# Four shared key neighbours, resident end blocks and whole-array value products in a sparse-attention and channel-mix kernel

## The chip, the cores and the metric

The kernel runs on one core of one Trainium2 chip. The metric is device time in microseconds (us) of one execution. The engines are named as in the profile: PE is TensorE (PEld its weight loads), DVE VectorE, ACT ScalarE, POOL GpSimd, SP SyncE, whose queue issues nearly all DMAs here.

## The reference

Inputs are `q`, `k`, `v` (4 batches, 8 heads, 768 positions, 64 channels, float32), three sampled key blocks for each of 24 query blocks of 32 positions, and the weights of a channel mixer.

```python
scores = (1 / np.sqrt(D)) * np.matmul(q, k.transpose(0, 1, 3, 2))
mask = np.abs(blk_i - blk_j) <= 1                       # a block and its neighbours
mask = mask | (blk_i == 0) | (blk_j == 0) | (blk_i == 23) | (blk_j == 23)
for qb in range(24):
    for kb in sampled_blocks[qb]:
        mask[qb*32:(qb+1)*32, kb*32:(kb+1)*32] = True
attn = softmax(np.where(mask, scores, -1e9)); x = attn @ v       # heads side by side: 512 channels
x_prev = x shifted by one position
xk = mu_k * x + (1 - mu_k) * x_prev;  xr = mu_r * x + (1 - mu_r) * x_prev
k = np.maximum(xk @ w_k, 0.0)                            # 512 -> 1024
out = sigmoid(xr @ w_r) * ((k * k) @ w_v)                # 1024 -> 512
```

The three weight matrices arrive as float64 and are taken apart on the chip.

## The kernel before, in words

Attention is done in 24 units (`UNITS`). Four of them are wide (`ALL`): for one batch, 128 queries of blocks 21, 22, 23 and 0 (the first and last block attend to everything, the others ride along under a mask) against all 768 keys. Twenty are near units `(pr, m)`: for a pair of batches, two neighbouring query blocks n = 2m+1 and n+1, so again 128 query rows (2 batches x 2 blocks x 32), each against 8 key blocks: its three window blocks, the first and the last block, and its three sampled blocks.

A wide unit goes head pair by head pair (`wide_pair`, four of them): scores of two heads (`sw`, L577, two row halves of the array side by side, 384 keys at a time), a fused mask-add-and-minimum on DVE (L494), an exponential on ACT (L504), twelve 128x128 transposes on PE (`tw`, L515), copied out four at a time (`ptw`, on ACT, L519), and the product with the values (L599). That product runs as four column tiles: for each of the 6 key chunks and each 32 queries there is a matmul of its own, with 32 stationary columns and the same 64 moving columns of values. Each float32 matmul is two PE instructions and two weight loads in the trace.

A near unit (`near_group`, twice, four heads each) does the same with 64x32 tiles for scores (`s`, L538), transposes (`t`, L515, copied out by DVE, L521) and 128x32 tiles for values (`o`, L560), where the four column tiles do have different values. `finish` divides by the sum (L621), transposes (`tx`, L618), and writes into `xt`, the mixer's input, by tiles of 256 positions.

Keys of a near unit sit in two tiles `KR0` and `KR1` of 8 blocks, one for each query block: three window blocks by one DMA from `kd` (L466), the two ends when the batch pair changes (L461), three sampled blocks by a DMA each from `kt` (L463). Both halves of the unit's scores read both tiles, so there is no second set to load into ahead of time. Values sit in a ring of six `VR` tiles of four blocks: for each query block a tile from `vw` (window and first block in one host-made table, L485) and one with the last block and the three sampled ones (`vt`, L480 and L482). A wide unit takes three of the same ring for its 768 keys (L440).

The mixer works on 12 tiles of 256 positions (`TILES`): `gate` (`r`, L744), `hidden` (`h_0`..`h_3`, L762), `values` (`v`, L791) as matmuls in three float32r terms of split operands; splitting is done on POOL, DVE and ACT (`split_x`, L707 to L720; `hidden`, L775 to L779). The 20 weight pieces are loaded on ACT's queue, rebuilt by ACT and three DVE steps (L360 to L373) and split on POOL (L383, L387).

Nothing of this runs in the order written. Every operation is added to a `Plan` with an engine, a cost in ns, a rank (a due time worked out from constants such as `A_STEP`, `M_STEP`, `O_PV`) and what it reads and writes. `Plan.order` simulates the engines with these costs and places at each step the operation with the lowest rank among those that can start soon; then everything is issued in that one order, and each engine's queue runs in order. Costs therefore decide the order, never the work. PE has modes in the plan: `whole`, `wide` (row halves), `scores` and `values` (small tiles), with a price `LEAVE` for leaving each. Where the plan sees a gap on PE of at least 150 ns before 95 us, it issues idle matmuls there (`spin`, L334, tile `idle`).

Of the kernel before, what the change touches and what calls it, by code (L numbers as in the profile page):

```python
# [29 lines left out]
QB, SLOTS = 4, 8  # L30
PAIR = 2
# [49 lines left out]
class Op:  # L81
    __slots__ = ("engine", "ns", "lag", "fn", "rank", "deps", "users", "bufs", "end", "start", "table", "seq", "waits", "release", "size", "parts", "ready")


class Plan:


    HOP = {"PE": 260, "ACT": 100, "DVE": 170, "POOL": 170, "SP": 60}
# [3 lines left out]
    RING, RATE, DONE, LANES = 650, 300, 670, 8  # L92
# [7 lines left out]
    def add(self, engine, ns, rank, fn, reads=(), writes=(), lag=0, table=None, release=0.0, size=0, parts=1):  # L100
# [5 lines left out]
        op.bufs, op.release, op.size, op.parts = [], release * 1000, size, parts  # L106
# [30 lines left out]
    def order(self):  # L137
        free, table, avail = {}, {}, {}
        queue_free = 0.0
        lanes, lane = [0.0] * self.LANES, 0  # L140
        for op in self.ops:
# [6 lines left out]
        while len(placed) < len(self.ops):  # L148
            best = None
            for engine, ops in avail.items():  # L150
                now = free.get(engine, 0.0)
                cand = []
                for op in ops:
                    at = max(now, op.ready)
                    for buf in op.bufs:
                        if not buf.taken:
                            slots, times, queue = self.queues[buf.tag]
                            if queue[0] is not buf or not times:
                                at = None
                                break  # L160
                            at = max(at, min(times)[0])
                    if at is not None:
                        cand.append((at, op))
# [25 lines left out]
            free[op.engine] = op.end  # L189
            for buf in op.bufs:  # L190
# [9 lines left out]
            for u in op.users:  # L200
                u.waits -= 1
                if not u.waits:
                    u.ready = max([u.release] + [d.end + (self.HOP[d.engine] if d.engine != u.engine else self.SAME.get(u.engine, 60)) + d.lag
                                                 for d in u.deps])
                    avail.setdefault(u.engine, []).append(u)
# [9 lines left out]
    (2, ALL), (0, ALL), (1, ALL), (0, 0), (0, 1), (0, 2), (0, 3), (3, ALL), (0, 4), (0, 5), (0, 6), (0, 7),  # L215
# [14 lines left out]
def block_sparse_attention_channel_mix(  # L230
    ctx: ExitStack, tc: tile.TileContext,
    kt, kd, kq, qw, qn, vt, vw, blocks, rows, consts, mu_k, mu_r, w_k, w_v, w_r, out, wide,
# [22 lines left out]
    KR = [fixed([P, SLOTS, PAIR, HP * BLK], F32, f"KR{i}") for i in range(KR_BUFS)]  # L255
# [11 lines left out]
    def mask_setup():  # L267
        own = buf([P, NM + 1, NRAND, 2], I32, "kk", 3, "own")
        con = buf([P, NM * (SEEN + SLOTS) + 2 * NB], F32, "zr", 3, "con")
        f = buf([P, NM + 1, NRAND], F32, "dif", 2, "ownf")  # L270
        same = buf([P, NM * NRAND * SEEN], F32, "x0", 1, "same")
# [18 lines left out]
        plan.add(DVE, 600, -15, pack, reads=[(number,)], writes=[(word,), (packed,)])  # L290
# [14 lines left out]
        def twice():  # L305
# [4 lines left out]
            e = same.ap.rearrange("p (a i b) -> p a i b", i=NRAND, b=SEEN)  # L310
# [3 lines left out]
            v.tensor_reduce(out=near_mask.ap[:, :, SEEN:], in_=e, axis=AX.X, op=ALU.max)  # L314
            d = same.ap[:, 0:NM].unsqueeze(2)
            for i, j in ((1, 0), (2, 0), (2, 1)):
                v.tensor_tensor(out=d, in0=g[:, :, i : i + 1], in1=g[:, :, j : j + 1], op=ALU.is_equal)
                m = near_mask.ap[:, :, SEEN + i : SEEN + i + 1]
                v.tensor_tensor(out=m, in0=m, in1=d, op=ALU.max)
            m = near_mask.ap[:, :, SEEN:]  # L320
            v.tensor_scalar(out=m, in0=m, scalar1=-FAR, scalar2=None, op0=ALU.mult)

        plan.add(DVE, 1100, -30, far, reads=[(own,), (con,)], writes=[(f,), (same,), (wide_mask,)])
        plan.add(DVE, 2400, TWICE, twice, reads=[(f,), (con,)], writes=[(same,), (near_mask,)])
# [20 lines left out]
    def weight(i, owner, key, dst, src, rank):  # L345
        f = buf([P, 512], F32, "zr", 3, f"wf{i}")
        if wide:
# [11 lines left out]
            else:  # L359
                plan.add(ACT, 600, rank, lambda: nc.scalar.activation(  # L360
# [16 lines left out]
            plan.add(DVE, 340, rank, shift, reads=[(mag,)], writes=[(mag,)])  # L377
            plan.add(DVE, 602, rank, sign, reads=[(mag,), (raw,)], writes=[(mag,)])
            plan.add(DVE, 602, rank, tail, reads=[(mag,), (raw,)], writes=[(f,)])
        else:  # L380
            plan.add(SP, ISSUE, rank, lambda: nc.sync.dma_start(f.ap, src), writes=[(f,)], size=262144)
        if i in HI_POOL:
            plan.add(POOL, 700, rank, lambda: nc.gpsimd.tensor_copy(dst()[:, 0, :], f.ap), reads=[(f,)], writes=[(owner, (0, key))])  # L383
        else:
            plan.add(ACT, 520, rank, lambda: nc.scalar.copy(dst()[:, 0, :], f.ap), reads=[(f,)], writes=[(owner, (0, key))])
        plan.add(POOL, 1230, rank,
# [20 lines left out]
    taken = [0, 0]  # L407

    def place(ring):

        taken[ring] += 1
        return (taken[ring] - 1) % (KR_BUFS, VR_BUFS)[ring]
# [7 lines left out]
    def load_wide(b, at):  # L420
# [13 lines left out]
        for i in range(NB // QB // 2):  # L434
            w = place(1)
# [9 lines left out]
    def load_near(pr, m, at):  # L445
# [4 lines left out]
        keys, values = [], []  # L450
        ahead = FIRST_K if (pr, m) == (0, 0) else LEAD_K
        for j in range(PAIR):
            n = PAIR * m + 1 + j
            r = place(0)
            keys.append(r)
            more = slots[0][r] != pr
            slots[0][r] = pr

            def fetch(r=r, n=n, more=more):
                if more:  # L460
                    nc.sync.dma_start(KR[r].ap[:, 3:5].rearrange("p n b x -> p n (b x)"), kt[pr * NB : (pr + 1) * NB : NB - 1].rearrange("n p x -> p n x"))  # L461
                for i in range(NRAND):
                    nc.sync.dma_start(KR[r].ap[:, 5 + i].rearrange("p b x -> p (b x)"),  # L463
                                      kt[bass.ds(sampled_block(n, i) + pr * NB, 1)].rearrange("o p x -> p (o x)"))

            plan.add(SP, ISSUE, at - ahead + 0.01 * j, lambda r=r, n=n: nc.sync.dma_start(  # L466
                KR[r].ap[:, 0:3].rearrange("p n b x -> p (n b x)"), kd[pr, :, n - 1 : n + 2].rearrange("p n x -> p (n x)")),
                writes=[(KR[r], "near")], release=at - ahead, size=393216)
            plan.add(SP, NRAND * FETCH + FIND * (pr == 0) + ISSUE * more, at - ahead + 0.01 * j, fetch, reads=[(packed,)],
                     writes=[(KR[r], "far")], release=at - ahead, size=131072 * (NRAND + 2 * more), parts=NRAND + more)  # L470
        for j in range(PAIR):
            n = PAIR * m + 1 + j
            near, far = place(1), place(1)
            values.append((near, far))
            more = slots[1][far] != pr
            slots[1][near], slots[1][far] = None, pr

            def gather(w=far, n=n, more=more):
                if more:
                    nc.sync.dma_start(VR[w].ap[0:BLK].rearrange("p b x -> p (b x)"), vt[(pr + 1) * NB - 1].rearrange("k b x -> k (b x)"))  # L480
                for i in range(NRAND):
                    nc.sync.dma_start(VR[w].ap[(i + 1) * BLK : (i + 2) * BLK].rearrange("p b x -> p (b x)"),  # L482
                                      vt[bass.ds(sampled_block(n, i) + pr * NB, 1)].rearrange("o k b x -> (o k) (b x)"))
# [3 lines left out]
            plan.add(SP, NRAND * FETCH + ISSUE * more, at - LEAD_V + 0.01 * j, gather, reads=[(packed,)],  # L487
                     writes=[(VR[far], 0, 1)], release=at - LEAD_V, size=131072 * (NRAND + more), parts=NRAND + more)
        return q, keys, values
# [13 lines left out]
    def exp(p, cs, keys, nm, col, L, h, rank):  # L503
        plan.add(ACT, 280 + 0.83 * (cs.stop - cs.start), rank, lambda: nc.scalar.activation(  # L504
# [3 lines left out]
    def turn(parts, name, rank, act=False):  # L508
# [9 lines left out]
        if act:  # L518
            plan.add(ACT, 490, rank + 0.1, lambda: nc.scalar.copy(pt.ap, tp.ap), reads=[(tp,)], writes=[(pt,)])  # L519
        else:  # L520
            plan.add(DVE, 600, rank + 0.1, lambda: nc.vector.tensor_copy(out=pt.ap, in_=tp.ap), reads=[(tp,)], writes=[(pt,)])  # L521
# [3 lines left out]
    ROWS = [slice(i * BLK, (i + 1) * BLK) for i in range(QB)]  # L525

    def near_group(b, m, gi, q, keys, values, o, L, t0):

        s = buf([P, 2, 512], F32, "s", 2, f"s{b}_{m}_{gi}", ps)
        p = buf([P, 4 * 256], F32, "p", P_BUFS, f"p{b}_{m}_{gi}")  # L530
        nm = buf([P, 4], F32, "nm", 4, f"nm{b}_{m}_{gi}")

        def mm():
            for a in range(2):
                hp = 2 * gi + a
                for j in range(QB):
                    for row, half in enumerate(HALF):
                        nc.tensor.matmul(  # L538
                            s.ap[ROWS[j], row, a * 256 : (a + 1) * 256].rearrange("p (n x) -> p n x", x=BLK),
                            q.ap[half, hp, ROWS[j]], KR[keys[j % PAIR]].ap[half, :, j // PAIR, hp * BLK : (hp + 1) * BLK],  # L540
                            start=True, stop=True, skip_group_check=True)

        plan.add(PE, 920, t0, mm, reads=[(q, 2 * gi, 2 * gi + 1), *[(KR[r], "near", "far") for r in keys]], writes=[(s,)], table="scores")
# [405 lines left out]
```

## Time and profile before

| | |
|---|---|
| median of 3 runs | 623.88 us (622.9 to 626.05) |
| the profiled execution | 623.73 us, span 622.0 us |
| PE busy | 589.5 us of the span, with 30.7 us of `idle` matmuls among them |
| DVE, ACT, POOL busy | 291.8, 301.0, 287.1 us |
| mean granted TensorE clock | 0.983 |
| DMA | 108.55 MB, mean 175 GB/s |

The busy time of PE counts an instruction to its modelled end, and consecutive matmuls overlap, so a group is best read from the start of its first instruction to the start of the next group, as the chain of waits gives it. Times of single instructions are longer than their share of a run of them: a 128x256 matmul of the mixer has a mean of 285 ns, and 24 of them take 3 us.

### The profile page before, as it was taken

The numbers are of one execution on the slowest core, as the hardware profiler recorded it, in microseconds if no ns is written. First come the engines' busy times: TensorE is split into PE (matmuls) and PEld (weight loads), VectorE is DVE, ScalarE is ACT, GpSimd is POOL, SyncE is SP. The second block draws the span as 40 slices with busy tenths as digits, with TensorE's granted clock in tenths as the row PEclk, the third lists the DMA queues.
The fourth block names the chain that finished last, engine by engine and source line by source line (L and its number), as shares of the span: only waits on it lengthen the run. The fifth ranks groups of instructions, "written<-read, shape, count | busy, mean of one in ns | idle before, by whom it ended". The sixth has DMA issues, their size and how long they took to land.

```text
span 622.0 us, 20533 instructions
## 1 busy us (share of the span) xinstructions
PE 589.5 (95%) x8267; PEld 479.7 (77%) x8281; DVE 291.8 (47%) x850; ACT 301.0 (48%) x716; POOL 287.1 (46%) x360
## 2 busy tenths in 40 slices
PE   9998898697989999899999999999999999999997
PEld 4666675465776897687887978979889788989896
DVE  5676764466688444734344343454343452312200
ACT  4676761356476355536273473554454554243341
POOL 1122411105475541564553653735617547496751
PEclk9999999799889999999999999999999999999999
DMA  8995799788679756885447447684384320000000
GB/s 323 337 322 195 212 246 261 214 284 280 190 208 279 239 144 174 264 228 153 167 141 224 124 132 214 182 265 136 111 257 136 120 79 2 35 17 18 18 18 34
DMA packets 54992, 108.55 MB, mean 175 GB/s; under 512 B 9681, under 2 KB 26706, under 8 KB 54898
## 3 DMA queue, kind: packets, MB, share of 16 engines
q1 hardware_dynamic: 51730, 96.63, 51.7%
q10 hardware_dynamic: 3168, 10.61, 5.1%
q8 instruction: 65, 1.06, 0.7%
q14 instruction: 29, 0.24, 0.1%
HBM read 100.40 MB, written 6.82 MB: 172 GB/s over the span
## 4 chain that ended last, share of the span: by engine, by line
PE 83%; DVE 6%; issue 5%; DMA 3%; SPq 2%; ACT 1%; ACTq 0%; DVEq 0%
PE v L791 20%; PE s L538 6%; PE r_0p L744 6%; PE o L560 5%; PE h_2p L762 5%; PE h_3p L762 5%; PE h_1p L762 5%; PE h_0p L762 5%; PE r_1p L744 5%; PE t L515 4%; PE tw L515 4%; PE sw L577 3%; PE idle L334 3%; DMA KR<-kt 2%; PE tx L618 2%
## 5 line engine op out<-in xcount | busy, mean ns | idle before, releaser
L791 PE MATMUL v<-wv,k 128*128 128x512 f32 (+1 forms) x600 | 137.9, 385 | 0.7 <-POOL wv L387 0.4
L791 PEld LDWEIGHTS v<-wv,k 128*128 128x128 f32 x600 | 107.8, 188 | 24.8 <-DVE z L799 1.4
L504 ACT ACTIVATE p<-p,nm 128x256 f32<-128x256 f32 x160 | 79.5, 499 | 29.4 <-DVE nm L494 29.1
L494 DVE CUSTOM_DVE_ANT_1 p<-s,near_mask 128x256 f32<-128x256 f32 x160 | 57.5, 421 | 56.7 <-PE s L538 48.1
L521 DVE COPY pt<-t 128x512 f32<-128x512 f32 x80 | 52.1, 684 | 36.7 <-PE t L515 36.5
L538 PE MATMUL s<-KR,q 64*32 64x256 f32 x1280 | 46.8, 399 | 8.9 <-issue 6.5
L720 POOL TENSOR_TENSOR xr<-xr_1f,xr 128x256 fp32r<-128x256 f32 x24 | 17.7, 736 | 67.0 <-ACT xr L718 66.7
L560 PEld LDWEIGHTS o<-VR,pt 128*32 128x32 f32 x2560 | 37.3, 110 | 11.0 <-issue 8.2
L560 PE MATMUL o<-VR,pt 128*32 128x64 f32 x2560 | 42.3, 220 | 3.5 <-issue 3.3
L515 PE MATMUL t<-ident,p 128*128 128x128 f32 x320 | 44.4, 280 | 0.3 <-PE tx L618 0.2
L515 PEld LDWEIGHTS t<-ident,p 128*128 128x128 f32 x320 | 38.3, 145 | 5.3 <-ACT p L504 1.1
L538 PEld LDWEIGHTS s<-KR,q 64*32 64x32 f32 x1280 | 24.4, 110 | 23.1 <-issue 14.7
L799 DVE SCALAR_TENSOR_TENSOR z<-v,z 128x512 f32<-128x512 f32 (+1 forms) x25 | 16.7, 668 | 50.8 <-PE v L791 29.5
L762 PE MATMUL h_3p<-xk,wk 128*128 128x256 f32 x288 | 38.6, 291 | 1.8 <-ACT h_2k L775 1.8
L762 PEld LDWEIGHTS h_3p<-xk,wk 128*128 128x128 f32 x288 | 36.3, 194 | 3.3 <-ACT h_2k L775 2.3
L762 PE MATMUL h_1p<-xk,wk 128*128 128x256 f32 x288 | 37.4, 285 | 1.3 <-ACT h_0k L775 1.3
L744 PE MATMUL r_0p<-wr,xr 128*128 128x512 f32 x144 | 37.9, 412 | 0.0
L519 ACT COPY ptw<-tw 128x512 f32<-128x512 f32 x48 | 26.6, 588 | 23.1 <-PE tw L515 17.7
L762 PE MATMUL h_2p<-xk,wk 128*128 128x256 f32 x288 | 37.5, 285 | 0.1
L762 PE MATMUL h_0p<-xk,wk 128*128 128x256 f32 x288 | 37.4, 285 | 0.2 <-ACT z L751 0.2
L762 PEld LDWEIGHTS h_2p<-xk,wk 128*128 128x128 f32 x288 | 35.4, 188 | 2.3 <-ACT h_1k L775 0.6
L762 PEld LDWEIGHTS h_1p<-xk,wk 128*128 128x128 f32 x288 | 35.2, 188 | 2.3 <-ACT h_0k L775 1.4
(131 smaller groups left out, 1033.5 us busy)
## 6 DMA issues: line engine op xcount, KB each, us to landing
VR<-vw SPq DMA_DIRECT2D x40, 512.0 KB, 5.6
VR<-vt SPq DMA_DIRECT2D x129, 128.0 KB, 5.3
KR<-kd SPq DMA_DIRECT2D x40, 384.0 KB, 4.2
KR<-kt SPq DMA_DIRECT2D x120, 128.0 KB, 3.8
k_ring<-kq SPq DMA_DIRECT2D x16, 384.0 KB, 5.8
VR<-vt SPq DMA_DIRECT2D x24, 256.0 KB, 6.6
out<-z SPq DMA_DIRECT2D x23, 256.0 KB, 2.6
q<-qn SPq DMA_DIRECT2D x20, 256.0 KB, 4.0
```

The costliest lines, as they stand in the source:

```text
L334: nc.tensor.matmul(idle.ap, one[:, 0:P], one, start=first and i == 0, stop=last and i == times - 1, skip_group_check=True)
L494: nc.vector.tensor_tensor_reduce(out=p.ap[:, cs].rearrange("p (a x) -> p a x", x=BLK), in0=view().rearrange("p (a x) -> p a x", x=BLK), in ...
L504: plan.add(ACT, 280 + 0.83 * (cs.stop - cs.start), rank, lambda: nc.scalar.activation(p.ap[:, cs], p.ap[:, cs], AF.Exp, bias=nm.ap[:, col ...
L515: nc.tensor.transpose(tp.ap[:, i, :], p.ap[:, cs], ident.ap)
L519: plan.add(ACT, 490, rank + 0.1, lambda: nc.scalar.copy(pt.ap, tp.ap), reads=[(tp,)], writes=[(pt,)])
L521: plan.add(DVE, 600, rank + 0.1, lambda: nc.vector.tensor_copy(out=pt.ap, in_=tp.ap), reads=[(tp,)], writes=[(pt,)])
L538: nc.tensor.matmul(s.ap[ROWS[j], row, a * 256 : (a + 1) * 256].rearrange("p (n x) -> p n x", x=BLK), q.ap[half, hp, ROWS[j]], KR[keys[j % ...
L560: nc.tensor.matmul(o.ap[ROWS[j], h * D : (h + 1) * D], pts[i // 2].ap[:, 2 * (i % 2) + g, ROWS[j]], VR[values[j % PAIR][g]].ap[:, j // PAI ...
L577: nc.tensor.matmul(s.ap[:, row, 0:W], q.ap[half, hp, :], K.ap[half, n0 * BLK : n0 * BLK + W], start=True, stop=True)
L744: nc.tensor.matmul(pr.ap[:, 0:512], xr.ap[:, a, c, :], wr.ap[:, w, c, :], start=(c == 0 and m == 0), stop=(c == CC - 1 and m == 2))
L762: nc.tensor.matmul(ph.ap[:, ff * TT : (ff + 1) * TT], wk.ap[:, w, c, f * P : (f + 1) * P], xk.ap[:, a, c, :], start=(c == 0 and m == 0), s ...
L791: nc.tensor.matmul(pv.ap[:, 0:width], k2.ap[:, a, f, i * P : (i + 1) * P], wv.ap[:, w, f, cs], start=(f == 0 and m == 0), stop=(f == FC - ...
```

## The change

- Keys: one tile `KR0` of 14 blocks instead of two of 8. In order: three sampled blocks of n, the two ends, the four blocks n-1 to n+2, the two ends again, three sampled blocks of n+1. Query block n reads the first 8, n+1 the last 8 (`WHERE`). One DMA loads the four neighbours, where two loaded three each. The mask's columns follow the new order.
- Values: the ring of six is split in three of one kind (sampled blocks and first block for n; window of n+1 and first block) and three of the other (last block and window, or sampled blocks). The end block stays in its tile until a wide unit takes it or the batch pair changes, and the window comes as 96 rows from `vt`; the table `vw` is gone.
- The wide product with the values is one matmul of 128 stationary columns for each key chunk, in mode `whole`, in place of four of 32. Its cost in the plan stays 700 ns for a head.
- Scores of all eight heads of a near unit are issued in a row, and so are their value products, from the sixth unit on (`MERGE`). The first needs two free `s` buffers, the second all four transposed tiles.
- Planned anew: costs of operations, hops between engines and all rank constants have new values, the plan now keeps DVE and POOL from some operations at the same time (`port`), of the three `ptw` copies of a head pair two stay on ACT and one goes to DVE, six of the twenty weight casts move from POOL to ACT, and the order of units differs.

```diff
 UNITS = [
-    (2, ALL), (0, ALL), (1, ALL), (0, 0), (0, 1), (0, 2), (0, 3), (3, ALL), (0, 4), (0, 5), (0, 6), (0, 7),
+    (2, ALL), (1, ALL), (0, ALL), (0, 0), (0, 1), (0, 2), (0, 3), (3, ALL), (0, 6), (0, 4), (0, 5), (0, 7),
...
-    KR = [fixed([P, SLOTS, PAIR, HP * BLK], F32, f"KR{i}") for i in range(KR_BUFS)]
+    KR = [fixed([P, SPAN, PAIR, HP * BLK], F32, f"KR{i}") for i in range(KR_BUFS)]
...
+        plan.add(SP, ISSUE, at - ahead, lambda: nc.sync.dma_start(
+            K.ap[:, WINDOW : WINDOW + 4].rearrange("p n b x -> p (n b x)"), kd[pr, :, n - 1 : n + 3].rearrange("p n x -> p (n x)")),
+            writes=[(K, "near")], release=at - ahead, size=524288)
...
-            plan.add(SP, ISSUE, at - ahead + 0.01 * j, lambda r=r, n=n: nc.sync.dma_start(
-                KR[r].ap[:, 0:3].rearrange("p n b x -> p (n b x)"), kd[pr, :, n - 1 : n + 2].rearrange("p n x -> p (n x)")),
-                writes=[(KR[r], "near")], release=at - ahead, size=393216)
...
+            def close(kind=near, w=w, j=j, more=more):
+                if more[kind]:
+                    end(kind, w)
+                nc.sync.dma_start(VR[w[kind]].ap[kind * BLK : (kind + 3) * BLK].rearrange("p b x -> p (b x)"),
+                                  vt[pr * NB + n + j - 1 : pr * NB + n + j + 2].rearrange("n k b x -> (n k) (b x)"))
...
-            plan.add(SP, ISSUE, at - LEAD_V + 0.01 * j, lambda w=near, n=n: nc.sync.dma_start(VR[w].ap.rearrange("p b x -> p (b x)"), vw[pr, n - 1]),
-                     writes=[(VR[near], 0, 1)], release=at - LEAD_V, size=524288)
...
+    WHERE = [slice(j * (WINDOW + 1), j * (WINDOW + 1) + SLOTS) for j in range(PAIR)]
+    def near_unit(b, m, together, q, keys, values, o, L, t0, t1):
...
+            op = plan.add(PE, 920, t0 if together else (t0, t1)[gi], mm, reads=[(q, 2 * gi, 2 * gi + 1), (keys, "near", ("far", 0), ("far", 1))],
+                          writes=[(s,)], table="scores", both="s" if together and not gi else None)
+            if together and gi:
+                op.rank -= 1000
...
+        groups = [(0, 1)] if together else [(0,), (1,)]
+        for mine in groups:
+            plan.add(PE, 920 * len(mine), (t0, t1)[mine[-1]] + O_PV, lambda mine=mine: [pv(gi) for gi in mine],
+                     reads=[(x,) for gi in mine for x in held[gi]] + [(VR[w], 0, 1) for two in values for w in two],
+                     writes=[(o, gi) for gi in mine], table="values")
...
             def pv(h=h, mine=mine):
                 for n, i in enumerate(mine):
-                    for j in range(QB):
-                        nc.tensor.matmul(
-                            o.ap[ROWS[j], h * D : (h + 1) * D], pts[i // 4].ap[:, i % 4, ROWS[j]],
-                            VR[values[n // 2]].ap[:, n % 2, h * D : (h + 1) * D], start=(n == 0), stop=(n == 5),
-                            skip_group_check=True)
+                    nc.tensor.matmul(
+                        o.ap[:, h * D : (h + 1) * D], pts[i // 4].ap[:, i % 4, :],
+                        VR[values[n // 2]].ap[:, n % 2, h * D : (h + 1) * D], start=(n == 0), stop=(n == 5),
+                        skip_group_check=True)
...
-KR_BUFS, VR_BUFS, P_BUFS, PT_BUFS, T_BUFS, M_BUFS = 2, 6, 4, 4, 2, 1
-T_ACT = ((0, 1, 2), (0, 1, 2))
+KR_BUFS, VR_BUFS, P_BUFS, PT_BUFS, T_BUFS, M_BUFS = 1, 6, 4, 4, 2, 1
+T_ACT = [[1, 2], [0, 1]]
+MERGE = 5
-HI_POOL = frozenset(range(20))
+HI_POOL = [2, 3, 4, 5, 6, 7, 8, 10, 13, 14, 15, 16, 17, 19]
-RAW_AT, RAW_GAP = -16.559, 8.229
+RAW_AT, RAW_GAP = -29.32, 8.577
-FIRST_K, LEAD_W, LEAD_Q, LEAD_K, LEAD_V = 32.834, 15.273, 22.533, 12.051, 10.413
+FIRST_K, LEAD_W, LEAD_Q, LEAD_K, LEAD_V = 26.425, 16.333, 21.82, 11.273, 9.889
-A_FIRST, A_WIDE, A_SOON, A_STEP = -6.908, 16.07, 11.323, 23.999
-SOON, SECOND = 8, 0.264
+A_FIRST, A_WIDE, A_SOON, A_STEP = -8.447, 16.128, 11.617, 27.197
+SOON, SECOND = 6, 0.502
-M_FIRST, M_STEP, M_LAST = 83.39, 40.819, 510.717
+M_FIRST, M_STEP, M_LAST = 80.518, 37.122, 508.53
```

The costs that change in the plan, with old and new values in ns: DVE's copy of four transposes 600 and 690, its fused mask step 345 and 430 for a near unit, 470 and 592 for a wide one, the three steps of a weight piece 340, 602, 602 and 425, 695, 695; ACT's copies 490 and 590. The costs on PE are as before.

More of the change, by code (lines that the diff above doesn't have):

```diff
@@ L81 @@
 class Op:
-    __slots__ = ("engine", "ns", "lag", "fn", "rank", "deps", "users", "bufs", "end", "start", "table", "seq", "waits", "release", "size", "parts", "ready")
+    __slots__ = ("engine", "ns", "lag", "fn", "rank", "deps", "users", "bufs", "end", "start", "table", "seq", "waits", "release", "size", "parts", "ready", "both", "port")
 class Plan:
-    HOP = {"PE": 260, "ACT": 100, "DVE": 170, "POOL": 170, "SP": 60}
+    HOP = {"PE": 270, "ACT": 50, "DVE": 60, "POOL": 70, "SP": 60}
     SWITCH = {"ACT": 1300}
@@ L140, in order @@
         lanes, lane = [0.0] * self.LANES, 0
+        port = {"DVE": 0.0, "POOL": 0.0}
+        other = {"DVE": "POOL", "POOL": "DVE"}
         for op in self.ops:
@@ L189, in order @@
             free[op.engine] = op.end
+            if op.port:
+                port[op.engine] = op.end
             for buf in op.bufs:
@@ L231, in block_sparse_attention_channel_mix @@
     ctx: ExitStack, tc: tile.TileContext,
-    kt, kd, kq, qw, qn, vt, vw, blocks, rows, consts, mu_k, mu_r, w_k, w_v, w_r, out, wide,
+    kt, kd, kq, qw, qn, vt, blocks, rows, consts, mu_k, mu_r, w_k, w_v, w_r, out, wide,
 ):
@@ L317, in twice @@
                 v.tensor_tensor(out=d, in0=g[:, :, i : i + 1], in1=g[:, :, j : j + 1], op=ALU.is_equal)
-                m = near_mask.ap[:, :, SEEN + i : SEEN + i + 1]
+                m = s_[:, :, i : i + 1]
                 v.tensor_tensor(out=m, in0=m, in1=d, op=ALU.max)
[L320 to L324, printed above, removed]
+            for j in range(PAIR):
+                m = near_mask.ap[:, :, j * SEEN : j * SEEN + NRAND]
+                x = stat + 2 * NB + j
+                v.scalar_tensor_tensor(out=m, in0=s_, scalar=c[:, x : x + 1], in1=m, op0=ALU.mult, op1=ALU.add)
+        plan.add(DVE, 1500, -30, far, reads=[(own,), (con,)], writes=[(f,), (same,), (wide_mask,)])
+        plan.add(DVE, 2600, TWICE, twice, reads=[(f,), (con,)], writes=[(same,), (near_mask,)])
         for w, m in enumerate((mu_k, mu_r)):
@@ L449, in load_near @@
                  writes=[(q, *range(HP))], release=at - LEAD_Q, size=262144)
-        keys, values = [], []
+        values = []
         ahead = FIRST_K if (pr, m) == (0, 0) else LEAD_K
-        for j in range(PAIR):
[L453 to L459, printed above, removed]
+        n = PAIR * m + 1
+        r = place_key()
+        K = KR[r]
+        more = slots[0][r] != pr
@@ L485, in load_near @@
-            plan.add(SP, ISSUE, at - LEAD_V + 0.01 * j, lambda w=near, n=n: nc.sync.dma_start(VR[w].ap.rearrange("p b x -> p (b x)"), vw[pr, n - 1]),
-                     writes=[(VR[near], 0, 1)], release=at - LEAD_V, size=524288)
-            plan.add(SP, NRAND * FETCH + ISSUE * more, at - LEAD_V + 0.01 * j, gather, reads=[(packed,)],
-                     writes=[(VR[far], 0, 1)], release=at - LEAD_V, size=131072 * (NRAND + more), parts=NRAND + more)
-        return q, keys, values
+            near, far = (1, 0) if j == 0 else (0, 1)
@@ L491, in soft @@
+            plan.add(SP, NRAND * FETCH + ISSUE * more[far], at - LEAD_V + 0.01 * j, gather, reads=[(packed,)],
+                     writes=[(VR[w[far]], 0, 1)], release=at - LEAD_V, size=131072 * (NRAND + more[far]), parts=NRAND + more[far])
+        return q, K, values
     def soft(s, view, table, mask, p, cs, nm, col, first, rank, ns):
@@ L698, in split_x @@
         dve = (b, t0 // TT) in DIF_DVE
-        engine, ns, sub = (DVE, 70 + 1.04 * tw, nc.vector) if dve else (POOL, 80 + 2.07 * tw, nc.gpsimd)
+        engine, ns, sub = (DVE, 70 + 1.04 * tw, nc.vector) if dve else (POOL, 195 + 1.63 * tw, nc.gpsimd)
         for h in range(CC // MIX):
@@ L908 @@
     twice = np.zeros((P, NM, SLOTS))
-    twice[:, :, 0] = np.where(row[:, 1:] == 1, -FAR, 0.0)
+    turned = (row[:, 1:] - 1) % PAIR
+    twice[:, :, SEEN] = np.where(row[:, 1:] == 1, -FAR, 0.0)
     blk = np.arange(NB)[None, :]
@@ L918 @@
     spare = ROOM - NB
-    window = np.array([[n - 1, n, n + 1, 0] for n in range(1, NB - 3)])
     arrays = {
```

196 lines of the change are left out of this document (108 added, 88 removed).

## The prediction

> **What bounds the kernel now.** I read first the page's busy time and its 40 slices, then the stretches of the span, then the chain of waits, last PE's weight loads.
>
> ```profile
> span 622.0 us, 20533 instructions
> PE 589.5 (95%) x8267; PEld 479.7 (77%) x8281; DVE 291.8 (47%) x850; ACT 301.0 (48%) x716; POOL 287.1 (46%) x360
> PEclk9999999799889999999999999999999999999999
> PE 83%; DVE 6%; issue 5%; DMA 3%; SPq 2%; ACT 1%; ACTq 0%; DVEq 0%
> ```
>
> PE is the bound: 95% busy, 83% of the chain that ended last. But the share is an average; by stretch (columns: length, then busy us of PE, PEld, DVE, ACT, POOL, then granted clock, DMA share and GB/s):
>
> ```profile
> 20.00:85.00 65.00, 58.06 (x1361) 41.13 (x1368) 45.30 (x142) 45.82 (x100) 17.47 (x18) 1.00 0.79 257
> 85.00:105.00 20.00, 19.51 (x401) 13.33 (x403) 11.67 (x33) 5.85 (x20) 3.76 (x4) 1.00 0.95 254
> 105.00:205.00 100.00, 83.35 (x1409) 62.99 (x1410) 68.08 (x187) 54.26 (x144) 41.10 (x50) 0.90 0.82 242
> 205.00:530.00 325.00, 321.67 (x4386) 273.10 (x4385) 140.57 (x421) 158.52 (x386) 167.98 (x212) 1.00 0.56 165
> ```
>
> Of this, the idle matmuls alone (same stretches, busy us of PE):
>
> ```profile
> 20.00:85.00 65.00, 8.02 (x30) 1.00 0.79 257
> 85.00:105.00 20.00, 9.77 (x41) 1.00 0.95 254
> ```
>
> From 205 us on PE hardly stops (321.67 of 325), and what is added to or taken from PE's work there moves the end one for one. Before, there is room: in 20 to 85 us 65 - 58.06 = 6.9 us not busy and 8.0 us of idle matmuls, in 85 to 105 us 0.5 and 9.8, in 105 to 205 us 16.7, at a clock of 0.90. That is 42 us in which real work could lie, if its inputs were there. The chain (start, length, what) shows how groups follow one another and where inputs were late:
>
> ```profile
> 58.32 1.48 PE o_-1_704 L599 x96
> 100.12 2.69 DMA KR<-kt
> 179.02 4.61 DMA raw<-w_v
> 187.28 4.56 DMA KR<-kt
> 253.00 4.27 DMA KR<-kt
> 303.26 1.03 PE o L560 x64
> 304.30 3.06 PE h_0p L762 x24
> 319.82 1.02 PE s L538 x32
> 330.26 1.92 PE o L560 x128
> 338.29 1.89 PE s L538 x64
> 592.97 2.87 PE h_0p L762 x24
> ```
>
> **The change, part by part.**
>
> *A. The wide product on the whole array: +16 us of PE work.* Now a head pair is 48 matmuls, 96 PE instructions, in 1.48 us (58.32): four column tiles at once, so 24 steps. At 24 steps of 64 columns that is at most 0.062 us a step. After the change 24 instructions remain, each with the same 64 moving columns, but with a weight load of 128 columns instead of four of 32 side by side. What such a load costs is seen at the start of groups, where the second load of the same rows follows the first before any matmul ends (PEld: start, length of the run, count):
>
> ```profile
> 146.24 0.30 PEld L577 LDWEIGHTS sw<-k_ring,qw 64*128 64x128 f32 x4 [0.17 <-issue]
> 162.59 0.30 PEld L762 LDWEIGHTS h_0p<-xk,wk 128*128 128x128 f32 x2 [0.39 <-ACT z L751]
> 147.73 0.20 PEld L515 LDWEIGHTS tw<-ident,pw 128*128 128x128 f32 x2 [0.55 <-ACT ptw L519]
> L577 PEld LDWEIGHTS sw<-k_ring,qw x128: 182/186/187, 6.8 to 147.0; 64*128 64x128 f32 x128
> L762 PEld LDWEIGHTS h_0p<-xk,wk 128*128 128x128 f32 x288 | 35.4, 188 | 1.5 <-issue 0.4 <-ACT z L751 0.4
> L515 PEld LDWEIGHTS tw<-ident,pw 128*128 128x128 f32 x192 | 22.0, 145 | 9.0 <-issue 3.0 <-ACT ptw L519 2.3 <-ACT pw L504 1.5
> ```
>
> A run of two loads that ends 0.30 us after its start, the second 0.187 long, means that loads start 0.11 us apart: in the wide scores (float32, four loads, two row halves at a time) and in the mixer (float32r). Transposes do it in 0.20 - 0.145 = 0.06 us. A matmul of 64 columns streams in about 0.06 us, so the load is the longer of the two, and loads in the background follow each other without a break: 24 x 0.11 = 2.64 us in place of 1.48, 1.16 us for a pair, 18.6 us for 16 pairs. Against that, no small tiles any more: an `h` group behind a small-tile group takes 3.06 us, one in the mixer's plain run 2.87, so 0.19 us goes where a product is followed by whole-array work. Not all are (wide scores are row halves): 0.15 x 16 = 2.4 us. Sum +16.2. Lower bound: loads at the transposes' 0.06 us, 24 x 0.06 = 1.44, and 16 x 0.19 saved: -3.7. Upper: the mixer's rate of a 256-column matmul with its load, 2.87 / 24 = 0.12: 24 x 0.12 = 2.88, +22.4. I take 0.11, since the wide scores are nearest: plain float32, 128 columns, the same unit.
>
> The Trainium skill ("TensorE: Matmul & The Clock Gate", section "LDWEIGHTS (loading the stationary operand)") gives a load's time as columns / 1.2 ns whatever the contraction, 107 ns for 128 columns. By it the pair would take 24 x 0.107 = 2.56 us, and the sum of A be about +15; the rows of wide scores and mixer agree, while the transposes' 0.06 us does not follow it. The rule speaks against this part.
>
> *B. How much of A is covered: -8 us.* Twelve of the 16 pairs lie before 85 us, four at 143 to 166 us (min, median and longest of an instruction, first and last start):
>
> ```profile
> L599 PE MATMUL o_-1_1139<-VR,ptw x384: 219/219/244, 69.2 to 83.0; 128*32 128x64 f32 x192
> L599 PE MATMUL o_-1_2404<-VR,ptw x384: 219/219/243, 143.3 to 166.3; 128*32 128x64 f32 x192
> ```
>
>  Before 85 us A adds 12 us, and PE has 6.9 us not busy. The idle matmuls are no cover by themselves: they are issued where the plan sees a gap, and it still prices a head at 700 ns, half of A's 1.3 us, so it sees gaps that aren't there. Every engine's queue runs in order, so late transposes and scores hold back the weight rebuilding on DVE behind them. In 85 to 205 us the delay meets waits for keys and weights that do not depend on it, and part vanishes. Ends: 0 and -16; I take the half, as PE's unused 6.9 us stand against 12 there.
>
> *C. Scores and products in a row: -4.5 us.* Two half groups of products take 2 x 1.03, one whole 1.92: 0.14 saved; of scores 2 x 1.02 against 1.89: 0.15. The group that followed the second half loses its 0.19 as well: 0.33 us a merge. Of 20 units about half have their halves together already (the rows at 330.26 and 338.29 against 303.26 and 319.82); 14 merges give 4.6. Ends: 0 (what is together already) and -6. The price: the second scores now need both `s` buffers, and behind them PE's queue waits; the merged product waits for all four `pt` copies, which is the whole ring of four, so the next unit's transposes can't be copied out, nor `finish` write its `x`, until it ran. After 205 us mixer groups stand between, each of 3 us, and cover it; before, the price lies in B's and E's ends.
>
> *D. Keys and values: -4 us.* Keys of a unit can only come when the unit before has done its scores; then SP issues (start, length):
>
> ```profile
> 178.30 0.36 SPq L466 DMA_DIRECT2D KR<-kd  x1
> 179.51 5.15 SPq L463 DMA_DIRECT2D KR<-kt  x3
> 184.75 0.38 SPq L466 DMA_DIRECT2D KR<-kd  x1
> 185.95 1.67 SPq L463 DMA_DIRECT2D KR<-kt  x3
> ```
>
> That unit's scores went on at 187.28 + 4.56. One `kd` issue goes: 185.95 - 184.75 = 1.2 us of SP's queue, and a sixth of the bytes (four blocks once for three twice, beside six sampled): 0.76 of 4.56. So 2 us for each of the three waits on the chain above: -6 at most, 0 if something else holds the queue, as a weight piece did at 179.02 (4.61 us), within the 5.15 us of three issues at 179.51. I take -4. With one tile in place of two nothing is lost: both halves read both tiles already.
>
> ```profile
> VR<-vw SPq DMA_DIRECT2D x40, 512.0 KB, 5.6
> VR<-vt SPq DMA_DIRECT2D x129, 128.0 KB, 5.3
> KR<-kd SPq DMA_DIRECT2D x40, 384.0 KB, 4.2
> ```
>
> In volume: `kd` 20 x 512 for 40 x 384 KB and values 40 x 384 for 40 x 512, 10.2 MB of 108.55 less; more end blocks for values (six tiles for each pair of batches and three again after the last wide unit, 15 for the 9 that 129 - 120 shows), 0.8 MB and six issues on SP. Values are on no step of the chain above: 0.
>
> *E. Planned anew: -4 us, the least known.* The old plan priced DVE and ACT short:
>
> ```profile
> L521 DVE COPY pt<-t 128x512 f32<-128x512 f32 x80 | 52.1, 684 | 36.7 <-PE t L515 36.5
> L494 DVE CUSTOM_DVE_ANT_1 p<-s,near_mask 128x256 f32<-128x256 f32 x160 | 57.5, 421 | 56.7 <-PE s L538 48.1 <-PE tw L515 8.6
> L519 ACT COPY ptw<-tw 128x512 f32<-128x512 f32 x48 | 26.6, 588 | 23.1 <-PE tw L515 17.7
> L383 POOL CAST wk<-wf 128x512 fp32r<-128x512 f32 x8 | 4.9, 612 | 43.0 <-DVE wf L373 43.0
> ```
>
> 600 for 684, 345 for 421, 490 for 588; the new prices fit. A queue order made with right prices should wait less where the order matters, in 105 to 205 us, with 16.7 us not busy. Ends: -12 (most of it filled) and +6 (A mispriced upsets it). Near zero is nearest, as units still depend on keys and weights there. Sixteen `ptw` copies move from ACT to DVE, 16 x 0.684 = 10.9 us, three quarters before 85 us: DVE 45.3 + 8.2 of 65 us, still under PE, which hides it. Six casts move from POOL to ACT, 6 x 0.6 = 3.5 us, where ACT loses 9.4: nothing. The unit order moves whole units of equal size: nothing.
>
> Sum: +16.2 - 8 - 4.5 - 4 - 4 = -4.3. The profiled execution took 623.73 us (span and 1.7 us around it), the median of the runs 623.88: 619.4, said as 619.
>
> **Rivals.**
> 1. *Slower: the product's loads stay uncovered.* PE's order is fixed with a price of half the true one, so idle matmuls and late copies stack up in the wide units: B is 0 and E 0. +16.2 - 4.5 - 4 = +7.7: 631. It decides once less than 4.6 us of A is covered with E at 0. For it: PE is 89% busy in 20 to 85 us. Against it: 27 us of idle and not busy time in 85 to 205 us.
> 2. *Faster by far: the early stretch closes up.* A is covered wholly, and the order with right prices and smaller loads fills part of the 16.7 us: 16.2 - 16 - 4.5 - 6 - 6 = -16: 608. For it: the clock of 0.90 there shows that PE starves. Against it: the starving is on keys and weights, and the weights' volume stays.
> 3. *A costs nothing*, loads run at the transposes' rate: -3.7 - 4.5 - 4 - 4 = -16: 607.
> 4. *No change: keys come no earlier.* The weights' transfers hold the queue as at 179.02, D is 0: 623.4.
>
> **How the numbers follow.** A measurement of this kernel tells a change from none at about 0.5%, 3.1 us. The case of the sum 0.33 (614 to 623; 0.24 of it faster by more than that, the rest within); rival 1 0.27 (0.24 slower); rival 2 0.21; rival 3 0.05; rival 4 0.14 (0.10 within, 0.04 slower). Faster 0.50, within 0.22, slower 0.28. The point is the sum's 619. The range 606 to 633 takes in rivals 2 and 1 and leaves out half of what lies beyond them.
>
> **What would show it.** A: `o` of L599's successor with 384 instead of 1536 PE instructions, and a pair in 2.6 us on the chain; 1.5 would be rival 3. B: the third wide unit ends later than 85 us, and idle matmuls are not fewer. C: score groups of 64 and product groups of 128 in most units, `h` groups of 3.06 us fewer. D: half as many `kd` issues, shorter waits for `KR` on the chain. E: more than 83.35 us of PE busy in 105 to 205 us, and a clock above 0.90. The prediction is wrong if the stretch after 205 us no longer runs without gaps, or if the wide units alone stretch by 15 us.

## The result and the profile after

The change makes the kernel slower: 644.71 us (638.76 to 647.47, four runs) against 624.04 us (622.9 to 626.05, four runs), a ratio of 1.0315, 95% interval 1.0238 to 1.0392. The profiled execution took 644.11 us. Where later ratios are compared, each is to the kernel before on the same chip (medians of 621 to 622 us there), so ratios, not times, are what carries over.

The page of the changed kernel: span, engines, the shares of the chain by line, and the DMA issues (count, KB each, median us to landing).

```profile
span 642.3 us, 18195 instructions
PE 608.7 (95%) x7130; PEld 502.4 (78%) x7142; DVE 296.0 (46%) x867; ACT 297.6 (46%) x706; POOL 283.5 (44%) x354
DMA packets 60903, 108.14 MB, mean 168 GB/s; under 512 B 10033, under 2 KB 36274, under 8 KB 60818
VR<-vt SPq DMA_DIRECT2D x135, 128.0 KB, 5.0
KR<-kt SPq DMA_DIRECT2D x120, 128.0 KB, 4.1
VR<-vt SPq DMA_DIRECT2D x40, 384.0 KB, 5.4
KR<-kd SPq DMA_DIRECT2D x20, 512.0 KB, 5.0
KR<-kt SPq DMA_DIRECT2D x40, 256.0 KB, 4.8
```

Two things are seen at once. PE is busy 19 us longer, in 1100 instructions fewer; 5.5 us of this are idle matmuls (36.2 us for 30.7). And the volume has hardly fallen: the loads from `kd` are halved as forecast, but there are 40 loads of 256 KB from `kt`, the two key ends, where 4 would do, as in the kernel before. The title of the change speaks of resident end blocks; for the keys the program doesn't keep them. The code has it in one name: `fetch` reads `more` when it is called, long after the loop for the values has set the same name to a list, and a list that isn't empty counts as true. The plan took its cost from the right value, so plan and program differ by 36 DMAs.

The wide product of the third unit (an instruction's shortest, median and longest time, first and last start), and two groups of the second unit's in the chain (start, length):

```profile
L642 PE MATMUL o_-1_864<-VR,ptw x96: 217/275/275, 78.8 to 96.5; 128*128 128x64 f32 x96
```

```profile
58.57 2.63 PE o_-1_590 L642 x24
66.30 1.29 PE o_-1_590 L642 x12
```

A pair takes 2.63 us (forecast 2.64), a quarter of the instructions, and the third wide unit ends at 96.5 us, not 83.0. The stretches of the changed kernel, to be read as the prediction's (length, busy us of PE, PEld, DVE, ACT, POOL, clock, DMA share, GB/s), and its idle matmuls:

```profile
20.00:85.00 65.00, 64.68 (x466) 49.62 (x471) 38.92 (x115) 32.53 (x65) 14.10 (x14) 1.00 0.66 214
85.00:105.00 20.00, 19.17 (x294) 15.84 (x294) 14.38 (x52) 12.96 (x39) 3.18 (x3) 1.00 0.79 206
105.00:205.00 100.00, 80.95 (x1316) 62.92 (x1319) 59.09 (x171) 45.19 (x125) 32.36 (x39) 0.93 0.89 252
```

```profile
20.00:85.00 65.00, 11.84 (x46) 1.00 0.66 214
105.00:205.00 100.00, 7.68 (x24) 0.93 0.89 252
```

Before 85 us PE has no room left (64.68 of 65), but 11.8 us of that are idle matmuls, 3.8 more than in the kernel before. From 105 to 205 us it is busy less than in the kernel before (80.95 for 83.35), though more work waits. The first `r` group tells when the mixer gets under way (first start behind the comma); in the kernel before:

```profile
L744 PE MATMUL r_0p<-wr,xr x144: 390/397/666, 123.4 to 592.6; 128*128 128x512 f32 x144
```

After:

```profile
L786 PE MATMUL r_0p<-wr,xr x144: 390/397/774, 143.7 to 614.5; 128*128 128x512 f32 x144
```

It is 20.3 us late, and the end of the span is 20.3 us late (642.3 for 622.0). Taken together the loss is there before 144 us. That says nothing yet of the parts: gains and losses behind the first `r` can cancel, and the runs below show that they do.

### The profile page after: what moved, and what is told of

The parts are those of the page before. It is cut to its first block, busy times and chain, and to the rows that moved or that the text cites. A ratio compares the mean times of both kernels' runs of the same rounds, so it can differ in the third digit from the quotient of the medians.

```text
span 642.3 us, 18195 instructions
## 1 busy us (share of the span) xinstructions
PE 608.7 (95%) x7130; PEld 502.4 (78%) x7142; DVE 296.0 (46%) x867; ACT 297.6 (46%) x706; POOL 283.5 (44%) x354
## 4 chain that ended last, share of the span: by engine, by line
PE 85%; DMA 8%; issue 3%; ACT 2%; SPq 1%; DVE 0%; ACTq 0%
PE v L833 20%; PE s L569 6%; PE r_1p L786 6%; PE r_0p L786 6%; PE o L600 5%; PE h_3p L804 5%; PE h_2p L804 5%; PE h_1p L804 5%; PE h_0p L804 5%; DMA raw<-w_v 4%; PE t L545 4%; PE idle L345 4%; PE sw L621 3%; PE tw L545 3%; DMA KR<-kt 2%
## 5 line engine op out<-in xcount | busy, mean ns | idle before, releaser
L569 PE MATMUL s<-KR,q 64*32 64x256 f32 x1280 | 45.4, 396 | 7.4 <-DMA KR<-kt 5.3
L786 PE MATMUL r_1p<-wr,xr 128*128 128x512 f32 x144 | 38.1, 415 | 3.7 <-ACT h_3k L817 3.7
L545 PEld LDWEIGHTS t<-ident,p 128*128 128x128 f32 x320 | 36.9, 141 | 5.7 <-DVE pt L551 1.3
L345 PE MATMUL idle<-const-bfloat16-1.0 128*128 128x512 bf16 x130 | 36.2, 414 | 1.6 <-PEq L942 0.8
```

What stands on the lines that cost most here:

```text
L345: nc.tensor.matmul(idle.ap, one[:, 0:P], one, start=first and i == 0, stop=last and i == times - 1, skip_group_check=True)
L545: nc.tensor.transpose(tp.ap[:, i, :], p.ap[:, cs], ident.ap)
L569: nc.tensor.matmul(s.ap[ROWS[j], row, a * 256 : (a + 1) * 256].rearrange("p (n x) -> p n x", x=BLK), q.ap[half, hp, ROWS[j]], keys.ap[half ...
L786: nc.tensor.matmul(pr.ap[:, 0:512], xr.ap[:, a, c, :], wr.ap[:, w, c, :], start=(c == 0 and m == 0), stop=(c == CC - 1 and m == 2))
```

## The experiments

Three theories: P, the product's weight loads cost the time; K, the key ends loaded again; O, the new order as such.

**The product tiled again**, in the changed order.

```diff
-                    nc.tensor.matmul(
-                        o.ap[:, h * D : (h + 1) * D], pts[i // 4].ap[:, i % 4, :],
+                    for j in range(QB):
+                        nc.tensor.matmul(
+                            o.ap[ROWS[j], h * D : (h + 1) * D], pts[i // 4].ap[:, i % 4, ROWS[j]],
```

> The changed kernel with the wide value product as four column tiles again, all operations in the changed order and with the changed plan. Theory P (the product's weight loads, 24 of 0.11 us for a pair in place of 1.48 us, uncovered): 16 pairs give back 1.15 us each and a little for mode changes is paid, so 644.7 falls by 14 to 20, to 625 to 631. Theory K (the key ends, which the changed kernel loads again for every unit: 40 loads of 256 KB where 4 were before) and theory O (the new order itself): at most 5 us, 640 or more, as the time would be lost to transfers or to the order.

629.16 us, ratio 1.0126 (1.0067 to 1.0185). P holds within the full change: 1.9 points of the ratio, some 12 us.

**The key ends staying**, the same order.

```diff
-            def fetch(j=j):
+            def fetch(j=j, more=more):
```

> The changed kernel with the key ends loaded only when the batch pair changes (4 loads of 256 KB, not 40), the same plan and order. Theory K: nine MB and 36 issues less, keys and weights land earlier in the stretch to 230 us, 632 to 638. Theory P: late inputs are not what costs the time, 642 to 645. Theory O: as P.

628.48 us, ratio 1.0119 (1.0092 to 1.0146): 2.0 points, some 12 us. K holds too, at the upper end of what was expected or a little above.

**Both edits.**

> Both of these edits: what is left of the change is the shared neighbours, resident ends, merged scores and products, and the new plan. P and K together: the parts add, 615 to 625, faster than before. Theory O: the order alone still costs, 630 or more. Should this be near 624, then merging, fewer bytes and the new plan together bring nothing.

618.62 us, ratio 0.9950 (0.9921 to 0.9980). The two faults together are 3.65 points of the ratio, some 23 us; what is left of the change is half a per cent faster than the kernel before. As the order of the operations is the same in these runs, O falls as the cause of the slowdown.

**The whole-array product alone, in the kernel before.**

```diff
-                    for j in range(QB):
-                        nc.tensor.matmul(
-                            o.ap[ROWS[j], h * D : (h + 1) * D], pts[i // 4].ap[:, i % 4, ROWS[j]],
+                    nc.tensor.matmul(
+                        o.ap[:, h * D : (h + 1) * D], pts[i // 4].ap[:, i % 4, :],
```

> The kernel before with only the wide value product on the whole array, its order untouched. Theory P: 16 pairs of 1.15 us longer, 638 to 643. If idle matmuls and waits of the early stretch cover it, as the prediction's term B had it for a half: 630 to 634. Theories K and O: near 624 to 628.

622.84 us, ratio 1.0030 (1.0004 to 1.0056). P's figure is far off: the same product that costs 10 to 12 us in the new order costs 2 us here, less than the half that the prediction allowed. The wide units do end later, but the first `r` group starts where it did (the `r` groups of this kernel and its third wide unit):

```profile
L743 PE MATMUL r_0p<-wr,xr x144: 390/397/505, 123.5 to 591.8; 128*128 128x512 f32 x144
L598 PE MATMUL o_-1_851<-VR,ptw x96: 219/275/275, 74.0 to 90.0; 128*128 128x64 f32 x96
```

90.0 instead of 83.0 us, and 123.5 instead of 123.4. The 7 us are swallowed between, mostly where the kernel before waits in the middle of groups (PE by time, idle time in front in brackets):

```profile
110.66 1.92 PE L538 MATMUL s<-KR,q 64*32 64x256 f32 x19 [3.37 <-issue]
121.34 0.86 PE L560 MATMUL o<-VR,pt 128*32 128x64 f32 x44 [2.30 <-issue]
```

The same two groups with the whole product:

```profile
113.66 1.92 PE L538 MATMUL s<-KR,q 64*32 64x256 f32 x51 [0.38 <-issue]
120.23 1.99 PE L560 MATMUL o<-VR,pt 128*32 128x64 f32 x128
```

A score group cut 3.37 us at its second half, a product group 2.30 us: with PE 7 us later the first is 0.38 and the second gone, which is 5.3 of the 7 us. The profile names no releaser for these waits; that they are for keys and values still on their way fits where the groups are cut, and is a reading of the trace.

**Bytes or issues.** Where the changed kernel loads the ends again, only 8 of 128 partitions are loaded.

```diff
-                if more:
-                    first = (END, WINDOW + 4)[j]
-                    nc.sync.dma_start(K.ap[:, first : first + 2].rearrange("p n b x -> p n (b x)"),
-                                      kt[pr * NB : (pr + 1) * NB : NB - 1].rearrange("n p x -> p n x"))
+                first, some = (END, WINDOW + 4)[j], P if fresh else 8
+                nc.sync.dma_start(K.ap[0:some, first : first + 2].rearrange("p n b x -> p n (b x)"),
+                                  kt[pr * NB : (pr + 1) * NB : NB - 1, 0:some].rearrange("n p x -> p n x"))
```

> The changed kernel; where it loads the key ends again for a unit of the same batch pair, it loads 8 of the 128 partitions: all 36 extra issues stay, 15 of 16 of their bytes go. Theory K-bytes (nine MB more, in rows of 1 KB, delay the keys and weights behind them): as with the ends staying, 628 to 632. Theory K-issues (36 more issues of 0.42 us and the gap behind each on SP's one queue): as the changed kernel, 640 to 645.

640.56 us, ratio 1.0317 (1.0248 to 1.0387), as the changed kernel's 1.0315 (1.0238 to 1.0392). Over the whole run the bytes cost nothing that can be measured, to about one point with these intervals; the issues carry the 12 us. On the way there it looks otherwise. The first `r` of this run:

```profile
L785 PE MATMUL r_0p<-wr,xr x144: 388/397/499, 136.8 to 611.3; 128*128 128x512 f32 x144
```

That is 6.9 us earlier than in the changed kernel (143.7) and only 1.5 us later than with the ends staying (135.3, shown below). Up to there most of the delay goes with the bytes: one product group waits 4.84 us in its middle in the changed kernel, 3.37 us here and 1.99 us with the ends staying. But the lead is gone soon after: the keys of the unit at 165 us are asked for at 165.45 us in the changed kernel and at 163.92 us here.

What two more issues do to a unit is seen in SP's queue for the third near unit's keys (start, length, line; the changed kernel):

```profile
102.93 0.37 SPq L473 DMA_DIRECT2D KR<-kd  x1
103.77 0.40 SPq L481 DMA_DIRECT2D KR<-kt  x1
105.00 2.31 SPq L484 DMA_DIRECT2D KR<-kt  x3
107.36 0.55 SPq L481 DMA_DIRECT2D KR<-kt  x1
108.92 1.84 SPq L484 DMA_DIRECT2D KR<-kt  x3
115.60 0.35 SPq L505 DMA_DIRECT2D VR<-vt  x1
```

With the ends staying:

```profile
103.36 0.37 SPq L473 DMA_DIRECT2D KR<-kd  x1
104.55 5.07 SPq L484 DMA_DIRECT2D KR<-kt  x6
111.01 0.35 SPq L505 DMA_DIRECT2D VR<-vt  x1
```

The unit's keys are issued in 7.83 us (102.93 to 110.76) in place of 6.26 (103.36 to 109.62), 1.57 us more for two issues, and each early unit's keys are asked for only when the one before has done its scores. From 85 to 235 us there are eight such units; for seven of them the two issues add 0.9 to 2.3 us, for one the time is 2.3 us shorter, in sum 7.7 us, some 0.5 us for an issue. That is most of the 12 us measured, not all of it. The delay does not grow evenly either: the sixth of these units has its first issue 7.9 us later than with the ends staying, the seventh 14.5 us. How much is an issue's own time and how much the wait for a place among the outstanding transfers (between 130 and 240 us SP waits 12.5 us for weight pieces in the changed kernel) was not separated.

**The reload in the kernel before.** `if more:` became `if True:` in its `fetch`.

> The kernel before, loading the key ends again for every unit (40 loads of 256 KB, not 4), order untouched. Theory K (the reload alone costs 10 to 16 us wherever it stands): 632 to 638. Rival: only the new order, whose early units follow one another closer, has no room for it: 622 to 627.

630.37 us, ratio 1.0182 (1.0124 to 1.0240). K costs 11 us there as well, near the lower end of the 10 to 16 us expected: the reload has its price in the old order too. Here the first `r` is not late at all (123.6 us for 123.4); all of it is lost behind.

```profile
L744 PE MATMUL r_0p<-wr,xr x144: 390/397/775, 123.6 to 598.9; 128*128 128x512 f32 x144
```

**No idle matmuls**, with ends staying and the whole product.

```diff
-SPIN_END, SPIN, SPIN_LEAST, SPIN_SHARE = 95.0, 213, 150, 1.5
+SPIN_END, SPIN, SPIN_LEAST, SPIN_SHARE = 95.0, 213, 1e9, 1.5
```

> The changed kernel with the key ends staying and the whole-array product (628.5 before this edit), without idle matmuls behind the first 20. Theory I (the 24 us of idle matmuls in 20 to 205 us, placed where a plan with the product at half its price saw gaps, take the room that the longer product needs): the product is covered, 617 to 621. Rival (they only fill waits, and keep the clock up): 628 or more, with a lower granted clock before 105 us.

619.88 us, ratio 0.9977 (0.9933 to 1.0022), from 1.0119: theory I (the idle matmuls take the room that the longer product needs) holds: they cost 1.4 points, 9 us. First start of `r` with the ends staying:

```profile
L786 PE MATMUL r_0p<-wr,xr x144: 388/397/499, 135.3 to 599.1; 128*128 128x512 f32 x144
```

Without idle matmuls as well:

```profile
L786 PE MATMUL r_0p<-wr,xr x144: 391/397/505, 124.9 to 590.2; 128*128 128x512 f32 x144
```

**The true price in the plan**: `plan.add(PE, 1340, ...)` for the product in place of 700, ends staying, idle matmuls as planned.

> The changed kernel with the key ends staying, and the whole-array product priced in the plan at 1340 ns for a head, not 700, planned again with the same constants. Theory I and the price: the plan sees fewer gaps, idle matmuls drop by 5 us or more, waits follow the true order: 618 to 624. If the price was harmless: 627 to 631. The constants were chosen for the old price, so a worse order is possible: above 632 would show that.

636.83 us, ratio 1.0283 (1.0223 to 1.0342): slower by 1.6 points, above 632, the miss that was named. The plan did put in fewer idle matmuls (14.7 us for 24.4 up to 205 us), and the order came out worse (idle matmuls of this kernel, then its first `r`):

```profile
20.00:85.00 65.00, 13.24 (x54) 1.00 0.70 232
85.00:105.00 20.00, 1.48 (x6) 1.00 0.69 188
```

```profile
L786 PE MATMUL r_0p<-wr,xr x144: 388/397/503, 147.8 to 609.1; 128*128 128x512 f32 x144
```

**No idle matmuls, the product tiled, ends staying.**

> The changed kernel with the product tiled again and the key ends staying (618.6 before this edit), without idle matmuls behind the first 20. Theory I (idle matmuls are in PE's way where PE sets the pace): with the shorter product there is more room, so less is won than the 8.6 us with the long one: 612 to 618. Rival (with short products PE is not what sets the pace before 105 us): 618 to 620, or slower by a lower clock.

615.02 us, ratio 0.9898 (0.9844 to 0.9952): the fastest kernel here, a per cent ahead of the kernel before. Against the whole product without idle matmuls (0.9977) the tiled one is still ahead by 0.8%, 5 us, though the two intervals overlap a little (0.9933 to 0.9952). So of the product's 10 us with ends staying, about half seems to stand on the idle matmuls.

**No idle matmuls in the kernel before.**

> The kernel before without idle matmuls behind the first 20, order untouched. If transfers set its pace in 85 to 125 us (its DMA share there is 0.95 and 0.81, and the long product cost it 1.3 us only): 620 to 624, nothing. Theory I everywhere: 612 to 617.

622.32 us, ratio 1.0042 (1.0000 to 1.0085): nothing won over the whole run, as expected. The reason expected, that transfers and not PE set the pace in 85 to 125 us, is not borne out: in the trace the first `r` starts at 115.9 us, 7.5 us earlier than with idle matmuls. The traced run is the fastest of twelve (618.47 us); where the others lose the lead again is not shown.

```profile
L744 PE MATMUL r_0p<-wr,xr x144: 390/397/505, 115.9 to 586.9; 128*128 128x512 f32 x144
```

**Keys and values alone.** The kernel before with one key tile, four shared neighbours, ends that stay, the values' two kinds and the new mask order; old costs and constants, planned again.

> The kernel before with the shared neighbours, the resident ends and the new mask order alone (one key tile, ends really staying, values ring in two kinds); product tiled, scores and products by halves, the old costs and constants, planned again with them. Theory S (SP's queue sets the early units' pace: one key issue less for a unit, nine MB less): 612 to 618. If the gain of the whole change minus its two faults (618.6 against 621.5) came from the new constants: 621 to 625.

625.80 us, ratio 1.0091 (1.0058 to 1.0124). Theory S falls in this form: fewer bytes and issues, and yet slower by 0.9%. Planned again with constants chosen for other transfers, the order on PE, DVE and ACT changed too, so this does not price the loads by themselves.

**No merging.** `MERGE = 99`, product tiled and ends staying, planned again.

> The changed kernel with the product tiled and the ends staying, but scores and products by halves in all units, planned again with the same constants. Prediction's term C (14 merges of 0.33 us): 621 to 625, slower than with merging. If the time saved by fewer mode changes is lost to transposes that wait for the four copies: 616 to 620. The order changes as well, so more than 6 us either way is the order's.

642.77 us, ratio 1.0346 (1.0289 to 1.0404): 24 us slower, which is the order's by the bound given beforehand, not that of mode changes. It tells nothing of merging; it tells how much the order can cost.

## Why the prediction was wrong

Forecast and runs side by side, in us (measured: the steps from 1.0315 by way of 1.0119 to 0.9950, times 624):

| | forecast | measured |
|---|---|---|
| the product (A and B) | +8.2 | +10.5 |
| key ends loaded again | not in the sum | +12.2 |
| all the rest (C, D, E) | -12.5 | -3.1 |
| sum | -4.3 | +19.6 |

The measured sum agrees with the 19.7 us of the whole change because the parts are differences along one path; by way of 1.0126 the product is 11.8 and the reload 11.0. The step that failed most is in D: it forecast fewer loads of keys and put a reload of the ends at nothing, going by the description of the change. The second is the rest of D with C and E, of which a quarter came. A and B together were off by 2 to 4 us.

**A, right in size.** 2.63 us a pair for 2.64; the row of the wide scores was the right one to take, and the transposes' rate (rival 3) was not met. The rule of the Trainium skill ("TensorE: Matmul & The Clock Gate", section "LDWEIGHTS (loading the stationary operand)") gave an estimate of 2.56, and the 2.63 of the trace agrees. The 2.4 us that A takes off for fewer mode changes were not measured by themselves.

**B, near in number, by a mean of two cases.** The prediction covered 8 of 16 us. In the changed kernel and with ends staying 4 to 6 were covered (the product costs 12 and 10.5 us there), in the kernel before nearly all (1.0030). Its signs came: the third wide unit ends late, and idle matmuls are not fewer. It named both mechanisms, idle matmuls that stay and waits that vanish, and took the half between them; that this lies near the new order's figure is luck. Which one rules depends on what is late behind the wide units: in the old order the added 7 us of PE work vanished in waits, for keys and values by the reading above; in the new order with ends staying PE itself was late, with 24 us of idle matmuls in the way (13.7, 3.3 and 7.4 in the three stretches), and taking these out gave 9 us back.

```profile
20.00:85.00 65.00, 13.73 (x54) 1.00 0.65 214
85.00:105.00 20.00, 3.32 (x13) 1.00 0.72 194
105.00:205.00 100.00, 7.35 (x28) 0.97 0.87 247
```

**D, the step that failed most.** -4 was forecast; the reload alone brought +12. The forecast counted one key issue less for a unit, by the change's description; the program has one less for `kd` and two more for the ends, so one more, because of the name `more`. This stood in the whole diff, though not in the parts of it shown above. No rival had it: rival 4's "keys come no earlier" went no further than zero. In kind D was partly sound: over the whole run the number of issues counts and the bytes do not (1.0317 for 1.0315), at some 0.5 us for an issue on the mean of eight units; up to the first `r` the bytes count as well. Whether the `kd` issue that was saved won anything is not shown by itself.

**C, not confirmed.** In a stretch from one first-`r` group to another, seven mixer tiles with ten units, the kernel before and the one with both edits have the same PE work, and merging shows no gain (length, then busy us and counts of PE and the other engines). The merging itself took place: all ten units have groups of 64 and 128 there, about half of them in the kernel before. The kernel before:

```profile
261.60:535.40 273.80, 272.52 (x3459) 232.09 (x3458) 113.35 (x342) 133.38 (x321) 144.99 (x185) 1.00 0.52 155
```

Both edits:

```profile
253.70:530.20 276.50, 272.53 (x3464) 233.22 (x3461) 111.66 (x333) 131.81 (x313) 143.89 (x182) 1.00 0.46 131
```

273.8 and 276.5 us. The time is not shorter. A part of the error is the 0.19 us that was to be saved with each mixer group that no longer stands behind small tiles: in the changed kernel's chain a group behind transposes (323.62) takes 2.94 us, not 2.87, one behind scores (336.10) 3.06, and transposes are what mostly comes instead. So 0.12 us is saved, not 0.19.

```profile
323.62 2.94 PE h_0p L804 x24
336.10 3.06 PE h_3p L804 x24
```

What holds up the rest was not tested by itself.

**E, not confirmed, and the widest.** -4 was taken between -12 and +6. What is left of the change without its two faults is 0.5% faster, so C, D's remainder and E together are some -3 us. E's sign, more than 83.35 us of PE busy in 105 to 205 us, did not come (80.95, and 82.08 with both edits). Three plans made again with unchanged constants came out 0.9%, 1.6% and 4% slower (keys and values alone, the true price, no merging) than the order they stem from. In each the content changed a little too, so the order's share is not priced; but an edit that moves the plan can cost more than what it edits.

**The sum.** Rival 1 had A uncovered, 631, and its mechanism was the nearest to what happened in the new order, where two thirds of A were uncovered. But it still gave C and D their -8.5 and knew nothing of the reload. The upper end of the range, 633, was worked out without a term for more loads, so it could not hold the 644.71.

## What to carry to other kernels

Count DMA issues in the program's own profile, not in its description: on a queue that serves units one after another, 36 issues more cost 12 us over the whole run whether they carried 256 KB or 16. In these traces a product step with 64 moving columns took as long as its load of 128 stationary columns (24 steps in 2.63 us, loads 0.11 us apart), and as four column tiles 0.062 us (24 steps in 1.48 us); this mattered just where PE was late. Work added to the bound engine can be nearly free where its neighbours are late (2 us for some 16 in the kernel before), so find out which of the two is late in that stretch before a cover is granted, and don't count filler work as room. And don't take an early milestone for the end: with narrow loads, and in the kernel before without idle matmuls, the first `r` came some 7 us earlier and the time was the same; with the ends loaded again in the kernel before it came no later and the time was 11 us longer.

## What the runs showed of the hardware that was not expected

That the bytes of 36 DMAs could be cut to a sixteenth with no effect on the whole time (1.0317 for 1.0315), though the first `r` came 6.9 us earlier. That a head's 12 instructions with 128 stationary and 64 moving columns take 1.29 us where 48 column-tiled ones took half of 1.48, though they are a quarter as many. And that without idle matmuls the granted clock fell in a stretch (tiled product, ends staying, 85 to 105 us: 0.83, with 13.65 us busy), and the kernel was the fastest nonetheless (length, busy us of PE, PEld, DVE, ACT, POOL, clock, DMA share, GB/s):

```profile
85.00:105.00 20.00, 13.65 (x351) 10.72 (x350) 12.31 (x45) 8.90 (x34) 3.15 (x3) 0.83 0.99 264
```
